# Two attentions with a gate on one core: the projections that come first are reordered and rerouted

## The chip, the cores and the metric

The kernel runs on one core of a Trainium2 chip. Its time is device time in microseconds (us), the median of three executions. Five engines with a queue each work side by side: PE (TensorE, matmuls, which read weights that PEld has loaded), DVE (VectorE), ACT (ScalarE), POOL (GpSimd) and SP (SyncE, here only a queue that issues DMA transfers). ACT and POOL can issue transfers too. An engine takes its instructions in the order in which they are written, and waits at one until its inputs are there.

## The reference

```python
def _A_ref(x, wqkv, wo):          # 32 heads, each with its own keys and values; D = 576, Dh = 18
    qkv = (x @ wqkv).reshape(B, S, 3, H, Dh).transpose(2, 0, 3, 1, 4)
    q, k, v = qkv[0], qkv[1], qkv[2]
    p = softmax(einsum("bhqd,bhkd->bhqk", q, k) * Dh ** -0.5)
    return einsum("bhqk,bhkd->bhqd", p, v).transpose(0, 2, 1, 3).reshape(B, S, D) @ wo

def _B_ref(x, wq, wk, wv, wo):    # 32 query heads share one key and one value
    q = (x @ wq).reshape(B, S, H, Dh).transpose(0, 2, 1, 3)
    k = x @ wk
    v = x @ wv
    p = softmax(einsum("bhqd,bkd->bhqk", q, k) * Dh ** -0.5)
    return einsum("bhqk,bkd->bhqd", p, v).transpose(0, 2, 1, 3).reshape(B, S, H * Dh) @ wo

x = A_x                            # 1 x 2048 x 576, float32
g = sigmoid((x * gate_w).sum(-1, keepdims=True))
return g * _A_ref(x, ...) + (1 - g) * _B_ref(x, ...)
```

## The kernel before

All numbers are float32. Where a matmul needs that accuracy, a matrix is cut into a rounded high part `h` and the rest, the low part `l`, and three products are summed: high by high, high by low, low by high.

**First phase (`project`, L205; the change lies here).** The columns of all query and key weights, of the shared value and of the gate stand side by side in `wall`, cut into 14 tiles (`mt`) of 128 columns. X transposed is 576 by 2048, in four chunks (`c`) of 512 positions, loaded as eight pieces `xs` of 256. A job (`mt`, `c`) is 14 matmuls into one PSUM bank. The contraction over 576 rows has four blocks of 128 and a fifth of 64, which `load5` (L127) loads twice, into both halves of the partitions. ACT rounds weights (`wh`, L133) and X (`xh`, L275); DVE makes the low parts (`wl`, L134; `xl`, L276; and for the fifth block L277, which puts the low part of X into the upper half of `xh`).

The products are kept as float16 pairs, scaled per row by powers of two in `tv`, so that queries and keys are of like size. For that `measure` (L159) takes the largest absolute weight of every column of a tile: a DVE reduction over the row blocks (`wabs`, L162), a PE transpose (L165) and another reduction (L166). `balance` (L168) masks these by what the columns are (`mask`, built in DRAM by small transfers and read back by an element gather), takes the largest of queries and keys and writes `tv` through a dozen small DVE steps and two small PE steps (L176, L183). It is called for the shared-key attention after tiles 0 to 4, and for the other after tiles 5 to 13.

The order: loads of W 0 to 4, then X; five measures; `balance(0, 5)`; then chunk by chunk tiles 0 and 1; then nine measures; `balance(2, 14)`; then tiles 2 to 13, each over its four chunks. A job's bank is evicted right behind its matmuls: ACT writes `ph` (L214) and, for tiles with keys, a copy `pst` (L217); DVE writes `pl` (L220); from tile 0 and the tiles with keys come differences of chunks too (`pd`, `pdh`, `pdl`, L223 to L226). `ph` is stored to DRAM (`qkh`) by ACT's queue, `pl` (`qkl`) by POOL's. `shared_v` (L236) turns the shared value of tile 0 with four PE transposes (L239). At its end the loads of the first keys (`ksb`, `kdb`) and queries (`qs`) wait on POOL.

**Lead and second phase.** The values are projected (`project_v`, L249, matmuls at L252) while the first row maxima are taken; its first matmul follows the last job on PE. Then, for 64 heads, scores, exponentials (ACT, L453), maxima (DVE, L418) and the products with values, in an order written out by hand, and the output product. These parts are the same in both kernels.

Of the kernel before, what the change touches and what calls it, by code (L numbers as in the profile page):

```python
# [49 lines left out]
def gated_mix_kernel(ctx: ExitStack, tc: tile.TileContext, xT, wall, wv, wo, out):  # L50
# [3 lines left out]
    def dma(o, i, eng=None):  # L54
        o, i = (x.bitcast(F32) if x.dtype == F32R else x for x in (o, i))
        return (eng or nc.sync).dma_start(o, i)  # L56
# [52 lines left out]
    def load_k(t, r, eng=None):  # L109
        load_rows(t, r, (0, 1, 0), eng)  # L110
# [13 lines left out]
        if l is not None:  # L124
            eng_l.tensor_tensor(l, src, h.bitcast(F32), op=OP.subtract)

    def load5(t, src):  # L127
        dma(t[:, 0:4, :], src[0:512, :].rearrange("(k p) m -> p k m", p=P))
        dma(t[0:64, 4, :], src[512:576, :])
        dma(t[64:128, 4, :], src[512:576, :])  # L130

    def split_w(st, w, eng_l):
        nc.scalar.activation(w["h"], st, AF.Copy)  # L133
        eng_l.tensor_tensor(w["l"], st, w["h"].bitcast(F32), op=OP.subtract)  # L134

    norm = wpool.tile([P, MT], F32, name="norm", bufs=1)
    tv = wpool.tile([P, MT], F32, name="tv", bufs=1)
    mask = wpool.tile([P, 4, MT], F32, name="mask", bufs=1)
    two = wpool.tile([2, P], F32, name="two", bufs=1)
# [4 lines left out]
    nc.gpsimd.memset(tv, 0.0)  # L144
    mask_d = dram.tile([4, MT * P], F32, name="mask_d")
# [8 lines left out]
    def load_w(mt):  # L154
        st = wpool.tile([P, NKT, P], F32, name="wst", bufs=MT)
        load5(st, wall[mt])
        return st

    def measure(mt, st):  # L159

        a = wpool.tile([P, P], F32, name="wabs")
        nc.vector.tensor_reduce(a, st.rearrange("p k f -> p f k"), axis=AX.X, op=OP.max,  # L162
                                apply_absolute_value=True)
# [4 lines left out]
    def balance(g, n):  # L168

        m = wpool.tile([P, 2, MT], F32, name="bm", bufs=1)  # L170
        for i in range(2):
            nc.vector.tensor_tensor(m[:, i, 0:n], norm[:, 0:n], mask[:, g + i, 0:n], op=OP.mult)
        r = wpool.tile([P, 2], F32, name="br", bufs=1)
        nc.vector.tensor_reduce(r, m[:, :, 0:n], axis=AX.X, op=OP.max)
# [6 lines left out]
        nc.vector.tensor_scalar(dg, ident[0:2, 0:2], x, None, op0=OP.mult)  # L181
        pb = ps_m.tile([P, 512], F32, name="pm")
        nc.tensor.matmul(pb[:, 0:2], two, dg, start=True, stop=True)  # L183
        b = wpool.tile([P, 2], F32, name="bb", bufs=1)
        nc.vector.reciprocal(b[:, 1:2], pb[:, 1:2])
        nc.vector.tensor_tensor(b[:, 0:1], pb[:, 0:1], b[:, 1:2], op=OP.mult)
        e = wpool.tile([P, 2], I32, name="be", bufs=1)
        nc.vector.tensor_single_scalar(e[:, 0:1], b[:, 0:1].bitcast(I32), 24, op=OP.logical_shift_right)
        nc.vector.tensor_scalar(e[:, 1:2], e[:, 0:1], 1.0, 64.0, op0=OP.mult, op1=OP.add)
        nc.vector.tensor_scalar(e[:, 0:1], e[:, 0:1], -1.0, 190.0, op0=OP.mult, op1=OP.add)  # L190
        t = wpool.tile([P, 2], F32, name="bt", bufs=1)
        nc.vector.tensor_single_scalar(t.bitcast(I32), e, 23, op=OP.logical_shift_left)
        nc.vector.tensor_scalar(t, t, LIFT, None, op0=OP.mult)
        for i in range(2):
            nc.vector.scalar_tensor_tensor(tv, mask[:, g + i, :], t[:, i:i + 1], tv, op0=OP.mult, op1=OP.add)

    def prep_w(st):
# [7 lines left out]
    def project(mt, c, w):  # L205

        fp = ps_s.tile([P, 512], F32, name="ps")
        cs = slice(c * 512, (c + 1) * 512)
        for n, (a, b, k, kr) in enumerate(PROJ):
            nc.tensor.matmul(fp, w[a][:kr, k, :], X[b][:kr, k, cs], start=(n == 0), stop=(n == len(PROJ) - 1))  # L210
# [10 lines left out]
        if c == 1 and mt in HAS_K:  # L221
# [2 lines left out]
            dh, dl = (stp.tile([P, 512], F16, name=f"pd{y}", bufs=1) for y in "hl")  # L224
            nc.scalar.activation(dh, d, AF.Copy, scale=t)
            nc.vector.scalar_tensor_tensor(dl, d, t, dh, op0=OP.mult, op1=OP.subtract)  # L226
        dma(qk_d[0][mt * P:(mt + 1) * P, cs], h, nc.scalar)
        dma(qk_d[1][mt * P:(mt + 1) * P, cs], l, nc.gpsimd)
        if c == 1 and mt in HAS_K:
            dma(kd_d[0][mt * P:(mt + 1) * P, :], dh, nc.scalar)  # L230
            dma(kd_d[1][mt * P:(mt + 1) * P, :], dl, nc.gpsimd)
        if mt == 0:
            dma(z_d[cs], st[ROW_G:ROW_G + 1, :], nc.scalar)
            return c, st

    def shared_v(c, st):  # L236
        pv = ps_m.tile([P, 512], F32, name="pm")
        for j in range(4):
            nc.tensor.transpose(pv[:, 18 * j:18 * j + 18],  # L239
# [20 lines left out]
            pass  # L260

    WV = []
    with tc.tile_pool(name="xs", bufs=6, side="right") as xsp:
        W = [load_w(mt) for mt in range(5)]
        XS = []

        def load_x(c):
            XS.append(xsp.tile([P, NKT, 256], F32, name="xs"))
            load5(XS[c], xT[:, 256 * c:256 * c + 256])

        def split_x(c):
            xs = XS[c]
            cs = slice(c * 256, (c + 1) * 256)
            xh = X["h"][:, :, cs]
            nc.scalar.activation(xh, xs, AF.Copy)  # L275
            nc.vector.tensor_tensor(X["l"][:, :, cs], xs[:, 0:4], xh[:, 0:4].bitcast(F32), op=OP.subtract)  # L276
            nc.vector.tensor_tensor(xh[64:128, 4], xs[64:128, 4], xh[64:128, 4].bitcast(F32), op=OP.subtract)  # L277

        for c in range(6):
            load_x(c)  # L280
        WP = [prep_w(W[0])]
        for mt in range(5):
            measure(mt, W[mt])
        balance(0, 5)
        for c in range(2):
            split_x(c)
        WP.append(prep_w(W[1]))
        for c in range(6, 8):
            load_x(c)
        for mt in range(5, MT):  # L290
            W.append(load_w(mt))
        for c in range(4):
            if c < 3:
                split_x(2 * c + 2)
                split_x(2 * c + 3)
            keep = project(0, c, WP[0])
            project(1, c, WP[1])
            shared_v(*keep)
    vwp = ph1.enter_context(tc.tile_pool(name="vwp", bufs=1, side="right"))
    VS = [vwp.tile([P, NKT, 288], F32, name="vwst"), None]  # L300
    load5(VS[0], wv[:, 0:288])

    for b in (SB, MB):
        dma(ksb[b + 54:b + 56, :], ones_r, nc.gpsimd)
    load_k(ksb, ROW_KB, nc.gpsimd)
    load_kd(kdb, ROW_KB, nc.gpsimd)
    load_q(0, nc.gpsimd)

    def project_rest():
        WN = prep_w(W[2])  # L310
        for mt in range(5, MT):
            measure(mt, W[mt])
        balance(2, MT)
        for mt in range(2, MT):
            w = WN
            if mt + 1 < MT:
                WN = prep_w(W[mt + 1])
            for c in range(4):
                project(mt, c, w)
            if mt in (4, 5):  # L320
                load_q(mt - 3, nc.gpsimd)
            if mt in (8, 11):
                hf = (mt - 8) // 3
                WV.append({y: vwp.tile([P, NKT, 288], F32R, name=f"vw{y}{hf}") for y in "hl"})
                split_w(VS[hf], WV[hf], nc.vector)
                if hf == 0:
                    VS[1] = vwp.tile([P, NKT, 288], F32, name="vwst")
                    load5(VS[1], wv[:, 288:576])

    project_rest()  # L330

# [444 lines left out]
```

## Time and profile before

| | us |
|---|---|
| median of three executions | 2733.3 (2733.19 to 2733.45) |
| the profiled execution | 2735.79 |
| its span | 2734.0 |
| PE busy | 2663.3 (97%) |
| DVE busy | 2430.7 (89%) |
| ACT busy | 2384.1 (87%) |
| POOL busy | 231.0 (8%) |
| granted clock of PE, mean | 0.991 |

A busy share is a mean over stages with different limits. The first 240 us, which hold the first phase, have another shape than the rest, and what the change is worth is read there. A row of a timeline gives start, duration, engine, line, instruction, output and input, and in brackets how long the engine stood idle before it and who released it.

### The profile page before, as it was taken

Reading aid. Unit: us, or ns where it says so; the run is one execution under the profiler, and the core shown is the slowest. Engines: PE = TensorE matmul, PEld = TensorE weight load, DVE = VectorE, ACT = ScalarE, POOL = GpSimd, SP = SyncE. Lnnn points to the kernel's source line nnn. Section 1 sums busy time; section 2 is a strip of 40 time slices with the busy share of each in tenths; the row PEclk is TensorE's granted clock in tenths of the full one; section 3 lists DMA queues with packets and bytes.
Section 4 is the critical chain, followed back from the end, with each engine's and each line's share of the span. In section 5 each row is a group of like instructions: output and inputs, shape, how many; then the busy total and the mean of one; then the engine's idle time right before and its main releaser. Section 6 shows DMA issues by size and latency. Waiting matters only on the chain.

```text
span 2734.0 us, 57725 instructions
## 1 busy us (share of the span) xinstructions
PE 2663.3 (97%) x22160; PEld 958.8 (35%) x22160; DVE 2430.7 (89%) x4582; ACT 2384.1 (87%) x4768; POOL 231.0 (8%) x438
## 2 busy tenths in 40 slices
PE   5899999999999999999999999999999999999999
PEld 3688522222222222222222333333333332223444
DVE  5345899999999999999999999999999999998875
ACT  3232499999999999999999999999999999998875
POOL 2221000001000200110110001000100020001000
PEclk9899999999999999999999999999999999999998
DMA  7232100001100100110132112112221122122312
GB/s 197 76 118 90 51 20 20 20 18 53 35 17 23 54 27 20 45 43 20 30 66 85 40 51 84 54 40 57 72 66 47 44 61 64 39 64 88 89 36 94
DMA packets 135321, 151.49 MB, mean 55 GB/s; under 512 B 55709, under 2 KB 104765, under 8 KB 133846
## 3 DMA queue, kind: packets, MB, share of 16 engines
q1 hardware_dynamic: 116156, 123.59, 16.2%
q10 hardware_dynamic: 14120, 13.65, 1.5%
q0 software_dynamic: 4768, 10.56, 1.2%
q8 instruction: 174, 2.85, 0.5%
q14 instruction: 103, 0.84, 0.1%
HBM read 92.02 MB, written 46.45 MB: 51 GB/s over the span
## 4 chain that ended last, share of the span: by engine, by line
ACT 54%; PE 37%; DVE 6%; DMA 2%; SPq 1%; issue 1%; DVEq 0%; ACTq 0%
ACT pt L453 48%; PE acc L459 12%; PE ps L446 11%; ACT xb L412 6%; PE ps L210 6%; PE pm L575 4%; DVE mx L418 3%; PE ps L252 2%; PE pm L409 2%; SPq L56 1%; DVE oe L469 1%; DVE junk L415 1%; DMA xs<-xT 0%; DVE oacc L629 0%; DVE oacc L583 0%
## 5 line engine op out<-in xcount | busy, mean ns | idle before, releaser
L453 ACT ACTIVATE pt<-ps 128x512 f32<-128x512 f32 x4052 | 2093.1, 637 | 68.4 <-PE pm L409 60.2
L418 DVE TENSOR_REDUCE mx<-pm 128x1 f32<-128x512 f32 x3096 | 1940.2, 682 | 89.5 <-PE pm L409 74.6
L446 PE MATMUL ps<-qs,ksb 56*128 56x512 f16 x2688 | 818.4, 380 | 10.8
L409 PE MATMUL pm<-ksb,qs 54*128 54x512 f16 x2364 | 738.5, 383 | 2.6 <-DVE mx L418 1.6
L459 PE MATMUL acc<-pt,vb 128*19 128x512 f32 (+1 forms) x6136 | 592.3, 458 | 1.9
L459 PE MATMUL acc<-pt,vg 128*19 128x256 f32 (+1 forms) x5664 | 579.5, 481 | 2.3 <-DVE oe L469 0.5
L409 PEld LDWEIGHTS <-qs 54*128 54x128 f16 x4096 | 330.0, 93 | 248.1 <-issue 195.2
L446 PE MATMUL ps<-qs,ksa 56*128 56x512 f16 x1364 | 404.4, 379 | 4.8 <-ACT pt L453 1.3
L446 PEld LDWEIGHTS <-ksb 56*128 56x128 f16 x2688 | 175.0, 94 | 622.5 <-issue 573.9
L409 PE MATMUL pm<-ksa,qs 54*128 54x512 f16 x1232 | 384.8, 382 | 0.6 <-ACT xb L412 0.4
L415 DVE CUSTOM_DVE_ANT_0 junk<-pm,xb 128x512 bf16<-128x512 f32 x500 | 339.9, 680 | 0.0
L412 ACT ACTIVATE xb<-pm 128x512 f32<-128x512 f32 x500 | 316.5, 633 | 0.0
L446 PEld LDWEIGHTS <-ksa 56*128 56x128 f16 x1408 | 89.3, 94 | 328.9 <-issue 299.0
L459 PEld LDWEIGHTS acc<-pt,vb 128*19 128x19 f32 x6136 | 104.1, 96 | 223.7 <-issue 206.6
L459 PEld LDWEIGHTS acc<-pt,vg 128*19 128x19 f32 x5664 | 96.0, 97 | 222.9 <-issue 204.9
L428 POOL TENSOR_SCALAR mt<-mt 128x32 f32<-128x32 f32 x64 | 18.6, 290 | 1616.4 <-DVE mt L426 1616.4
L214 ACT ACTIVATE ph<-ps,tv 128x512 f16<-128x512 f32 x56 | 38.5, 687 | 122.0 <-PE ps L210 114.5
L409 PE MATMUL pm<-kdb,qs 54*128 54x512 f16 x372 | 141.5, 380 | 0.0
L220 DVE SCALAR_TENSOR_TENSOR pl<-ps,tv,ph 128x512 f16<-128x512 f32 x56 | 42.0, 751 | 93.8 <-ACT ph L214 75.4
L210 PE MATMUL ps<-xh,wh 128*128 128x512 f32 x280 | 76.4, 403 | 3.3 <-DVE xh L277 2.6
L210 PE MATMUL ps<-xh,wl 128*128 128x512 f32 x280 | 75.1, 399 | 0.0
L469 DVE COPY oe<-acc 128x512 f32<-128x512 f32 x63 | 43.6, 692 | 30.0 <-PE acc L459 29.4
(123 smaller groups left out, 1253.8 us busy)
## 6 DMA issues: line engine op xcount, KB each, us to landing
qs<-qkh SPq DMA_DIRECT2D x244, 72.0 KB
qs<-qkl SPq DMA_DIRECT2D x122, 72.0 KB
onh<-oh SPq DMA_DIRECT2D x32, 256.0 KB
onl<-ol SPq DMA_DIRECT2D x32, 256.0 KB
oih<-onh SPq DMA_DIRECT2D x16, 512.0 KB
oil<-onl SPq DMA_DIRECT2D x16, 512.0 KB
ot<-oe SPq DMA_DIRECT2D x220, 36.0 KB
R<-r_d SPq DMA_DIRECT2D x55, 144.0 KB
```

The lines of the kernel that those rows point to most:

```text
L210: nc.tensor.matmul(fp, w[a][:kr, k, :], X[b][:kr, k, cs], start=(n == 0), stop=(n == len(PROJ) - 1))
L220: nc.vector.scalar_tensor_tensor(l, fp, t, h, op0=OP.mult, op1=OP.subtract)
L252: nc.tensor.matmul(fp[:, 0:288], X[b][:kr, k, st_ * P:(st_ + 1) * P], w[a][:kr, k, :], start=(n == 0), stop=(n == len(PROJ) - 1))
L409: nc.tensor.matmul(pm, qs[u % 3][b:b + 54, i * P:(i + 1) * P], k, start=True, stop=True)
L412: nc.scalar.activation(MX["x", u, i], pm, AF.Relu)
L415: nc.vector.tensor_tensor_reduce(junk, pm, MX.pop(("x", u, i)), 1.0, -3e38, op0=OP.add, op1=OP.max, accum_out=MX[u][:, i, c:c + 1])
L418: nc.vector.tensor_reduce(MX[u][:, i, c:c + 1], pm, axis=AX.X, op=OP.max)
L446: nc.tensor.matmul(ps, kst(u)[b:b + 56, i * P:(i + 1) * P], qs[u % 3][b:b + 56, c * 512:(c + 1) * 512], start=True, stop=True)
L453: nc.scalar.activation(pt, ps, AF.Exp, scale=SCALE / LIFT ** 2)
L459: nc.tensor.matmul(acc[32 * j:32 * j + 19, a:b], v_of(u, i), PT[u, i, j][:, a:b], start=(i == 0 and a == 0), stop=(i == 15), skip_group_ch ...
L469: nc.vector.tensor_copy(oe, acc)
L575: nc.tensor.matmul(fp[:, 0:288], o[b][:r, t, s2 * P:(s2 + 1) * P], w[a][:r, t, 288 * hf:288 * hf + 288], start=(n == 0), stop=(n == 3 * nt ...
```

## The change

- Three tiles go through X chunk by chunk instead of two (`JOBS`). W 0, X 0, W 1, X 1, W 2 are loaded in this order, X 0 by ACT's queue. For the first chunk the three tiles are multiplied a 256-column half at a time. 18 matmuls on zeros run ahead of them, and a small ACT instruction ahead of the first weights.
- `measure` falls into `measure_b` (tiles 0 to 4: one largest value a partition for the queries and one for the shared keys) and `measure_a` (tiles 4 to 13: a value a column and partition, kept), both without PE. `balance` does the rest over partitions at once, in three parts between which jobs 4 and 5 (or 14 and 15) stand. The first two chunks' six banks (three `ps`, three `pm`) are held until the first balance has ended.
- From then on the eviction of a job is written behind the matmuls of the next (`late`, `flush`); banks alternate by threes between the two pools. The measures of tiles 4 to 13 stand between the evictions of jobs 7 to 13.
- The 64-row block is loaded once; ACT writes its rounded weights to both halves.
- The mask is loaded by rows and turned by four PE transposes.
- `ph`, `pdh` and the gate's row are stored by POOL, as `pl` is; from tile 3 on, POOL makes the low weights.
- The loads of the first keys and queries stand between jobs of tiles 4 to 7.

The number of jobs (56) and of matmuls in one (14) is as before.

```diff
-PROJ = [("h", "h", k, 128) for k in range(NKT)] + [("h", "l", k, 128) for k in range(NKT - 1)] + \
-       [("l", "h", k, 128) for k in range(NKT)]
+PROJ = [("h", "h", k, 128) for k in range(NKT - 1)] + [("l", "h", k, 128) for k in range(NKT - 1)] + \
+       [("h", "l", k, 128) for k in range(NKT - 1)] + [("h", "h", NKT - 1, 128), ("l", "h", NKT - 1, 64)]
...
-    def load5(t, src):
-        dma(t[:, 0:4, :], src[0:512, :].rearrange("(k p) m -> p k m", p=P))
-        dma(t[0:64, 4, :], src[512:576, :])
-        dma(t[64:128, 4, :], src[512:576, :])
+    def load5(t, src, eng=None):
+        dma(t[:, 0:4, :], src[0:512, :].rearrange("(k p) m -> p k m", p=P), eng)
+        dma(t[0:64, 4, :], src[512:576, :], eng)
...
-        nc.scalar.activation(w["h"], st, AF.Copy)
-        eng_l.tensor_tensor(w["l"], st, w["h"].bitcast(F32), op=OP.subtract)
+        nc.scalar.activation(w["h"][:, 0:4], st[:, 0:4], AF.Copy)
+        for b in (0, 64):
+            nc.scalar.activation(w["h"][b:b + 64, 4], st[0:64, 4], AF.Copy)
+        eng_l.tensor_tensor(w["l"][:, 0:4], st[:, 0:4], w["h"][:, 0:4].bitcast(F32), op=OP.subtract)
+        eng_l.tensor_tensor(w["l"][0:64, 4], st[0:64, 4], w["h"][0:64, 4].bitcast(F32), op=OP.subtract)
...
-    dma(mask, mask_d.rearrange("g (m p) -> p g m", p=P), nc.gpsimd)
+    dma(mask_r, mask_d.rearrange("g (m p) -> m g p", p=P), nc.gpsimd)
+
+    def turn_mask():
+        pt = ps_m.tile([P, 512], F32, name="pm")
+        for g in range(4):
+            nc.tensor.transpose(pt[:, MT * g:MT * g + MT], mask_r[:, g, :], ident[0:MT, 0:MT])
+        nc.vector.tensor_copy(mask, pt[:, 0:4 * MT].rearrange("p (g m) -> p g m", m=MT))
...
-    def measure(mt, st):
-        a = wpool.tile([P, P], F32, name="wabs")
-        nc.vector.tensor_reduce(a, st.rearrange("p k f -> p f k"), axis=AX.X, op=OP.max,
+    def size(n, st):
+        for k0, k1, p in ((0, 4, P), (4, 5, 64)):
+            nc.vector.tensor_reduce(n[0:p, k0 // 4:k0 // 4 + 1], st[0:p, k0:k1], axis=AX.XY, op=OP.max,
+                                    apply_absolute_value=True)
+    def measure_b(mt, st):
+        if mt == 0:
+            size(norm_b[:, 0, 0:2], st[:, :, ROW_KB:ROW_KB + DH])
+        f0, f1 = max(ROW_Q - P * mt, 0), min(ROW_Q + DH * H - P * mt, P)
+        size(norm_b[:, 1, 2 * mt:2 * mt + 2], st[:, :, f0:f1])
+    def measure_a(mt, st):
+        o = norm_a[:, P * (mt - 4):P * (mt - 3)]
+        nc.vector.tensor_reduce(o, st[:, 0:4].rearrange("p k f -> p f k"), axis=AX.X, op=OP.max,
                                 apply_absolute_value=True)
-        pt = ps_m.tile([P, 512], F32, name="pm")
-        nc.tensor.transpose(pt[:, 0:P], a, ident)
-        nc.vector.tensor_reduce(norm[:, mt:mt + 1], pt[:, 0:P], axis=AX.X, op=OP.max)
+        a = wpool.tile([64, P], F32, name="wabs", bufs=1)
+        nc.vector.tensor_reduce(a, st[0:64, 4:5].rearrange("p k f -> p f k"), axis=AX.X, op=OP.max,
+                                apply_absolute_value=True)
+        nc.vector.tensor_tensor(o[0:64], o[0:64], a, op=OP.max)
...
-        w = {y: wpool.tile([P, NKT, P], F32R, name=f"w{y}") for y in "hl"}
-        split_w(st, w, nc.vector)
+        w = {y: wpool.tile([P, NKT, P], F32R, name=f"w{y}", bufs=4) for y in "hl"}
+        split_w(st, w, eng or nc.gpsimd)
...
-        dma(qk_d[0][mt * P:(mt + 1) * P, cs], h, nc.scalar)
+        dma(qk_d[0][mt * P:(mt + 1) * P, cs], h, nc.gpsimd)
         dma(qk_d[1][mt * P:(mt + 1) * P, cs], l, nc.gpsimd)
...
+    def project(n, hold=False):
+        mt, c = JOBS[n]
+        fp = bank(n // 3 % 2)
+        products(fp, WP[mt], 512 * c, 0, 512)
+        if not hold:
+            flush()
+        late.append(lambda: evict(mt, c, fp))
+        if mt == 0:
+            late.append(lambda: late.append(lambda: shared_v(c)))
...
+        FP = [bank() for mt in range(3)]
+        for i in range(2):
+            for mt in range(3):
+                products(FP[mt], WP[mt], 0, 256 * i, 256 * i + 256)
+        for mt in range(3):
+            measure_b(mt, W[mt])
+        for c in (2, 3):
             split_x(c)
+        turn_mask()
...
+        for mt in (3, 4):
+            measure_b(mt, W[mt])
+        project(3, hold=True)
+        bal = balance(0)
+        for n in (4, 5):
+            next(bal)
+            project(n, hold=True)
+        run(bal)
+        for mt in range(3):
+            evict(mt, 0, FP[mt])
+            if mt == 0:
+                for c in (4, 5):
+                    split_x(c)
+        flush()
+        WP.append(prep_w(W[3]))
+        shared_v(0)
+        for n in range(6, 12):
+            if n == 8:
+                for c in (6, 7):
+                    split_x(c)
+            project(n)
+            for mt in range(*AT.get(n, (0, 0))):
+                measure_a(mt, W[mt])
```

What the change moves, in the order of the instructions, at three places.

PE, the start of the first phase. Before: five transposes of measures (L165), the balance (L176, L183), then tiles 0 and 1 on chunk 0.

```order
L165 MATMUL pm<-ident,wabs 128x128 x5
L176 MATMUL pm<-ident,br 2x128
L183 MATMUL pm<-bd,two 128x2
L210 MATMUL ps<-xh,wh 128x512 x5
L210 MATMUL ps<-xl,wh 128x512 x4
L210 MATMUL ps<-xh,wl 128x512 x5
```

Now, from the end of job 4 on: a step of the balance (L205), job 5 (L240, banks `pm`), the other step (L213), the shared value's transposes (L276) and job 6.

```order
L240 MATMUL pm<-xh,wh 128x512
L240 MATMUL pm<-xh,wl 128x512
L205 MATMUL pm<-ident,br 2x128
L240 MATMUL pm<-xh,wh 128x512 x4
L240 MATMUL pm<-xh,wl 128x512 x4
L240 MATMUL pm<-xl,wh 128x512 x4
L240 MATMUL pm<-xh,wh 128x512
L240 MATMUL pm<-xh,wl 128x512
L213 MATMUL pm<-bd,two 128x2
L276 MATMUL pm<-ident,pst 128x18 x4
L240 MATMUL ps<-xh,wh 128x512 x4
```

The products no longer stand behind the balance; the first eviction does.

DVE, around the measures of the later tiles. Before: behind the last eviction of tiles 0 and 1 (L220), the low weights of tile 2, and nine pairs of a measure and its second reduction.

```order
L220 SCALAR_TENSOR_TENSOR pl<-ps,tv,ph 128x512 x2
L242 COPY vb<-pm 128x4x18
L134 TENSOR_TENSOR wl<-wst,wh 128x640
L162 TENSOR_REDUCE wabs<-wst 128x128
L166 TENSOR_REDUCE norm<-pm 128x1
L162 TENSOR_REDUCE wabs<-wst 128x128
L166 TENSOR_REDUCE norm<-pm 128x1
```

Now, from the eviction of job 6 (L254) on: the measures of tiles 4 and 5 (L186 to L191), then the last two pieces of X (L333, L334), then job 7 and the next measure.

```order
L254 SCALAR_TENSOR_TENSOR pl<-ps,tv,ph 128x512
L186 TENSOR_REDUCE norm_a<-wst 128x128
L189 TENSOR_REDUCE wabs<-wst 64x128
L191 TENSOR_TENSOR norm_a<-norm_a,wabs 64x128
L186 TENSOR_REDUCE norm_a<-wst 128x128
L189 TENSOR_REDUCE wabs<-wst 64x128
L191 TENSOR_TENSOR norm_a<-norm_a,wabs 64x128
L333 TENSOR_TENSOR xl<-xs,xh 128x4x256
L334 TENSOR_TENSOR xh<-xs,xh 64x256
L333 TENSOR_TENSOR xl<-xs,xh 128x4x256
L334 TENSOR_TENSOR xh<-xs,xh 64x256
```

The measures moved in between the evictions, two of them ahead of the last pieces of X.

POOL, around the loads of the third head's queries (`qs_94`). Before: the low stores (`qkl`, and `kdl` for a difference) and the loads.

```order
L56 DMA qkl<-pl 128x512 x2
L56 DMA kdl<-pdl 128x512
L56 DMA qkl<-pl 128x512 x2
L56 DMA qs_94<-qkh 18x2048 x2
L56 DMA qs_94<-qkl 18x2048
```

Now: both stores of each job, and the low weights of the next tile (L136, L137) between them.

```order
L56 DMA kdh<-pdh 128x512
L56 DMA kdl<-pdl 128x512
L56 DMA qkh<-ph 128x512
L56 DMA qkl<-pl 128x512
L136 TENSOR_TENSOR wl<-wst,wh 128x512
L137 TENSOR_TENSOR wl<-wst,wh 64x128
L56 DMA qkh<-ph 128x512
L56 DMA qkl<-pl 128x512
L56 DMA qs_94<-qkh 18x2048 x2
L56 DMA qs_94<-qkl 18x2048
```

POOL's queue now holds all stores of a job and half of the weight split.

More of the change, by code (lines that the diff above doesn't have):

```diff
@@ L304, in gated_mix_kernel @@
         dma(ksb[b + 54:b + 56, :], ones_r, nc.gpsimd)
-    load_k(ksb, ROW_KB, nc.gpsimd)
-    load_kd(kdb, ROW_KB, nc.gpsimd)
-    load_q(0, nc.gpsimd)
     def project_rest():
[L310 to L328, printed above, removed]
+        bal = None
@@ new lines, in project_rest @@
+        for n in range(12, len(JOBS)):
+            mt, c = JOBS[n]
+            if c == 0 and mt + 1 < MT:
+                WP.append(prep_w(W[mt + 1]))
+            project(n)
+            for m in range(*AT.get(n, (0, 0))):
+                measure_a(m, W[m])
+            if n == 13:
+                bal = balance(2)
+            if n in (13, 14):
+                next(bal)
+            if n == 15:
+                run(bal)
+            if c == 0:
+                if mt == 4:
+                    load_k(ksb, ROW_KB, nc.gpsimd)
+                    load_kd(kdb, ROW_KB, nc.gpsimd)
+                if mt == 5:
+                    load_q(0, nc.gpsimd)
+                if mt in (6, 7):
+                    load_q(mt - 5, nc.gpsimd)
+                if mt in (7, 10):
+                    hf = (mt - 7) // 3
+                    VS[hf] = vwp.tile([P, NKT, 288], F32, name="vwst")
+                    load5(VS[hf], wv[:, 288 * hf:288 * hf + 288])
+                if mt in (9, 12):
+                    hf = (mt - 9) // 3
+                    WV.append({y: vwp.tile([P, NKT, 288], F32R, name=f"vw{y}{hf}") for y in "hl"})
+                    split_w(VS[hf], WV[hf], nc.vector)
@@ L330, in gated_mix_kernel @@
+        for f in list(late):
+            f()
     project_rest()
```

108 lines of the change are left out of this document (66 added, 42 removed).

## The prediction

> A difference of 0.2% (5.5 us of 2733) is about what a measurement of this kernel can tell from no change.
>
> **What bounds the kernel now.** I read the page's slices first, then the busy time by stretch, then the chain of waits of the first 320 us. The slices show where TensorE is not full:
>
> ```profile
> PE   5899999999999999999999999999999999999999
> DVE  5345899999999999999999999999999999998875
> ACT  3232499999999999999999999999999999998875
> ```
>
> Each digit is a slice of 68 us. Only PE's first three are below 9; from the fifth on ACT and DVE are full, and that part is not edited. The stretches (busy us of PE, PEld, DVE, ACT, POOL; granted clock; DMA share; GB/s):
>
> ```profile
> 0.00:23.80 23.80, 3.27 (x8) 1.49 (x8) 10.35 (x24) 4.58 (x5) 7.37 (x19) 1.00 0.77 164
> 23.80:238.50 214.70, 192.82 (x812) 154.45 (x813) 98.59 (x149) 70.67 (x99) 49.81 (x94) 0.94 0.39 123
> 60.00:62.00 2.00, 0.00 (x0) 0.00 (x0) 1.36 (x2) 1.23 (x2) 1.97 (x4) 0.61 0.95 244
> ```
>
> The projections end at 238.5, DVE and ACT below half busy, Pool a quarter. In the chain (start, us, what) PE's stretches and what separates them:
>
> ```profile
> 22.95 5.08 DMA xs<-xT
> 28.52 7.91 PE ps L210 x24
> 57.50 4.07 DMA wst<-wall
> 61.59 5.93 DMA vwst<-wv
> 67.56 1.23 DVE wabs L162
> 82.02 156.70 PE ps L210 x672
> 238.72 3.73 PE ps L252 x28
> ```
>
> The last 48 of the 56 products are back to back: 672 matmuls in 156.70 us. PE waits in two places: until 23.8 for weights, X and the first balance, and from 57.7 to 82 for nine measures and the second balance. The timeline shows both, and the clock:
>
> ```profile
> 6.57 1.28 ACT L133 ACT_TABLE_LOAD   x1 [6.57 <-DMA wst<-wall]
> 23.83 2.07 PE L210 MATMUL ps<-xh,wh 128*128 128x512 f32 x4 [0.66 <-ACT xh L275]
> 57.24 0.42 PE L239 MATMUL pm<-ident,pst 18*128 18x18 f32 x4
> 81.44 0.58 PE L183 MATMUL pm<-bd,two 2*128 2x2 f32 x2 [0.80 <-DVE bd L181]
> 81.95 2.50 PE L210 MATMUL ps<-xh,wh 128*128 128x512 f32 x5
> 82.06 0.17 DVE L185 RECIPROCAL bb<-pm 128x1 f32<-128x1 f32 x1 [0.67 <-PE pm L183]
> 83.42 0.50 DVE L195 SCALAR_TENSOR_TENSOR tv<-mask,bt,tv 128x14 f32<-128x14 f32 x2
> 87.94 1.32 PE L210 MATMUL ps<-xh,wh 128*128 128x512 f32 x5
> ```
>
> The job at 81.95 takes 6.0 us to 87.94, at half clock. Taking its excess out, a warm job of 14 matmuls costs (156.70 - 2.8)/48 = 3.2 us, so a cold start costs 2.8. All 56 need 179 us; the rest of 238.7 is what the change can reach, some 59 us.
>
> **The change part by part.** Durations of one instruction, from the groups kept apart by shape (busy total, mean ns):
>
> ```profile
> L162 DVE TENSOR_REDUCE wabs<-wst 128x128 f32<-128x640 f32 x14 | 17.1, 1223 | 0.0
> L134 DVE TENSOR_TENSOR wl<-wst,wh 128x640 fp32r<-128x640 f32 x14 | 11.5, 824 | 10.8 <-ACT wh L133 10.7
> L276 DVE TENSOR_TENSOR xl<-xs,xh 128x1024 fp32r<-128x1024 f32 x8 | 9.8, 1224 | 1.9 <-ACT xh L275 1.7
> L277 DVE TENSOR_TENSOR xh<-xs,xh 64x256 fp32r<-64x256 f32 x8 | 3.4, 422 | 0.2
> L220 DVE SCALAR_TENSOR_TENSOR pl<-ps,tv,ph 128x512 f16<-128x512 f32 x56 | 42.0, 751 | 93.8 <-ACT ph L214 75.4 <-ACT pst L217 18.4
> L226 DVE SCALAR_TENSOR_TENSOR pdl<-pd,tv,pdh 128x512 f16<-128x512 f32 x10 | 7.5, 752 | 7.9 <-ACT pdh L225 7.9
> L214 ACT ACTIVATE ph<-ps,tv 128x512 f16<-128x512 f32 x56 | 38.5, 687 | 122.0 <-PE ps L210 114.5 <-DMA wst<-wall 5.1 <-PE pm L239 2.1
> L217 ACT ACTIVATE pst<-ps 128x512 f32<-128x512 f32 x13 | 7.7, 590 | 0.0
> L133 ACT ACTIVATE wh<-wst 128x640 fp32r<-128x640 f32 x14 | 10.2, 734 | 4.2 <-ACT ph L214 3.2 <-DMA wst<-wall 0.9
> L275 ACT ACTIVATE xh<-xs 128x1280 fp32r<-128x1280 f32 x8 | 10.0, 1269 | 14.8 <-DMA xs<-xT 13.9 <-ACT ph L214 1.0
> L56 POOL DMA_DIRECT2D qkl<-pl x56 | 30.5, 545 | 161.0 <-DVE pl L220 150.8 <-DVE vb L242 5.7 <-DVE pdl L226 4.1
> L125 POOL TENSOR_TENSOR ol<-ot,oh 128x512 fp32r<-128x512 f32 x32 | 40.9, 1277 | 5.3 <-DMA onl<-ol 3.8
> L239 PE MATMUL pm<-ident,pst 18*128 18x18 f32 x16 | 1.7, 215 | 0.0
> ```
>
> Front. The table load moves ahead of the weights. They land at 6.6, their split (0.73, in three pieces 1.1) ends at 7.7 and X's first piece (1.27) at 9.0, so the first product starts at 9.0 instead of 23.8. X now shares this time with the weights; 384 columns of 576 floats, 0.9 MB, must have come:
>
> ```profile
> 4.00:6.00 2.00, 0.00 (x0) 0.00 (x0) 0.00 (x0) 0.00 (x0) 1.63 (x4) 1.00 0.69 183
> 22.00:24.00 2.00, 0.72 (x3) 0.67 (x4) 1.01 (x7) 1.49 (x2) 0.00 (x0) 1.00 1.11 294
> ```
>
> At 294 GB/s from 4 us on this costs nothing; at 183 the later steps slip by 1 to 4 us (two pieces and three weights, 896 columns, 2.06 MB, at 15.3 instead of 11). I take the fast one, since the row at 4 has weights alone, at the pace at which SP issued them.
>
> Chunk 0 is done in six half groups of 14 matmuls on 256 columns. Half a job is 1.6 us; the L252 row gives 1.87 for 14 on 288 columns (3.73 for 28). I take 1.75: to 19.5, with the mask's turn 20.0. DVE keeps ahead: three weight splits of 0.82 and two X pieces of 1.22 + 0.42 from 7.4 on end at 13.2, before the second half's 14.3. Then come five tiles' measures without a transpose (three of them first: 1480 elements at no more than L162's 1.9 ns, 2.8 us, and four 64-row ones of some 0.25) and two X pieces, at 20.3; job 3 needs them at 21.8. The 18 empty products before 9.0 only set the clock. Jobs 3 to 5: 9.6, and 0.4 for a transpose: 30.0.
>
> The stall that stays. Nothing can be evicted before the balance, whose last part follows job 5. Its PE part (0.58) and DVE tail (82.06 to 83.92: 1.9) end at 32.5. Then ACT does 0.69 + 0.59 for the first bank and the two X pieces of chunk 2 (1.27 each, now in two instructions: 2.6) before job 6 can start: 36.4. PE stands 5.8 us. In the stretch 60:62 the mean clock is 0.61, so it fell to half near 60.4, 2.8 us after the last matmul (57.24 + 0.42); so here too it falls, and job 6 starts cold: 2.8, or 2.4 as in the 24 matmuls of 7.91 (5.5 warm). I take 2.6; without the fall it is 0. The Trainium skill ("TensorE: Matmul & The Clock Gate", Part 1) has the gate close after an idle window of about 3.4 us that runs free of the kernel, which would close it here as well, and a window at half clock costs half of it, an estimate of 1.7 us, by which the sum were 0.9 lower; the trace's 2.4 to 2.8 decides.
>
> Jobs 6 to 55: 50 x 3.2 = 160.3 (3.206 before rounding). What lies beside them: ACT 0.69 a job, now one job late and with no job waiting for it, since a bank returns after six. In the way: three times four turns of V (0.4 each), 1.2; the second balance's two small PE steps, 1.0; and DVE. From 32.5 it owes, until job 9 needs chunk 3 at 50.8, seven low parts (5.3), the difference and its low part (1.5), four X pieces (6.6), two measures (0.98 for 512 of L162's 640 elements and two small steps of some 0.25: 1.45 each) and copies (0.4), 16.7 us in 18.3 with hand-overs from ACT: wait 0 to 3, I take 1. Then six low parts (4.5), eight measures (11.6) and two reductions with a copy (1.7) until the second balance's transpose after job 14, at 69.6; from 51.8 on they end at 69.6 too: wait 0 to 2, I take 0.5. Together 3.7. So the nine measures' 14 us of waiting, the loads ahead of them and the second cold start go.
>
> Pool. It takes over the high stores and the weights' low parts. A tile has ten issues (5.45), 1.28 for the low part and 0.25 to 1.3 for its 64 rows: 7.0 to 8.0 of 12.8 us. Its last store frees the bank's copy three jobs later:
>
> ```profile
> qkl<-pl POOLq DMA_DIRECT2D x56, 128.0 KB, 2.1
> ```
>
> At 2.1 us to land there are 6 us of slack; a tile's low part is needed four jobs after it is made. Cost: nothing, while Pool needs less than 3.2 us a job. The 64-row loads drop a third of the issues of SP.
>
> Sum: 36.4 + 2.6 + 160.3 + 3.7 = 203.0 instead of 238.7: 35.7 us less. The rest follows with the same instructions. The profiled execution took 2735.79 (its span 2734.0), 2.5 above the median of 2733.3; from the median: 2697.6, say 2698.
>
> **The rivals.** *DVE's debt.* If ACT's hand-overs or the measures are longer, X's last pieces come late, job 9 waits and the clock falls again. Price: 5 us of wait, 2.8 cold, 2 more at the second balance, 10 us: 2708. For it: 16.7 of 18.3 us; against: later there is slack.
>
> *Pool locked out by DVE.* If Pool's issue must wait for the DVE instruction that runs, a store takes up to 0.545 + 1.22. Two stores (3.5) and a quarter of a low part (0.4) make 3.9 us a job, 0.7 over PE's, for the dozen jobs in which DVE is full: 8.8 us, 2707. The row that bears on it:
>
> ```profile
> 61.38 1.22 DVE L162 TENSOR_REDUCE wabs<-wst 128x128 f32<-128x640 f32 x1
> 61.59 0.52 POOL L56 DMA_DIRECT2D ksb<-qkh  x1
> ```
>
> This issue lies wholly inside a DVE reduction and takes no longer than others, so I give it little. The Trainium skill ("SBUF — State Buffer", "SBUF: two separate sides") warns of such a lock, in which DMAs issued from GpSimd wait while VectorE runs a two-port instruction; by that rule the stores were better left on ACT's queue, and no row here shows it.
>
> *The front fed late.* With all loads at 183 GB/s and latencies on top, chunks 0 and 1 end 10 us later, with two cold starts between: 15.6, 2713.
>
> *Pool the bound (slower).* All stores now stand in one queue. If a high store there costs not 0.545 but what the mask's gather cost Pool,
>
> ```profile
> L56 POOL DMA_DIRECT2D mask<-mask_d x1 | 2.6, 2555 | 2.6 <-DMA mask_d<-zo 2.6
> ```
>
> a tile with five of them needs 12.8, 2.7 for the others and 1.6 for the low part, 17.1 us, 4.3 a job: 50 jobs take 54 us more, 2752. It decides from 0.71 us a job above 3.2, where the gain is gone (35.7/50). Against it: that gather had 4-byte pieces, and the same store of the low part takes 0.545.
>
> **How the numbers follow.** Forecast 0.66, alone 2693 (no fall of the clock, no wait of DVE, half groups at 1.6) to 2707 (slow loads 4, waits at their upper ends 3.5, 2 for hand-overs between engines). DVE's debt 0.13, Pool locked 0.07, front late 0.06; the change without effect, since something else starts the next stage at 238.7, 0.02; Pool the bound 0.06. The range 2688 to 2713 adds below one cold start (2.8) that a shift in time may spare the second stage, and leaves out the last two and some of the tails. Faster 0.92, same 0.02, slower 0.06.
>
> **What would show it.** Right: first product near 9, one hole of 5 to 6 us near 31 with half clock behind it, the first product of V (now L289) near 203, Pool's stores at 0.55. Wrong: holes between jobs 16 and 55, Pool above 3 us a job, or the second phase longer than 2495 us.

## The result, and the profile after

The changed kernel takes 2725.8 us (median of 9 runs, 2725.0 to 2726.2) against 2733.3 (9 runs of the kernel before on the same chip): a ratio of 0.9972, 95% interval 0.9962 to 0.9982. That is 7.5 us less, where 35 were forecast (2698, range 2688 to 2713). The profiled execution took 2726.2, its span 2724.3.

The slices of the page, PE, DVE and ACT. PE's first slice has an 8 for a 5, the second a 9 for an 8:

```profile
PE   8999999999999999999999999999999999999999
DVE  6335899999999999999999999999999999998865
ACT  4332599999999999999999999999999999998875
```

So TensorE is busy nearly everywhere, and the time is still only 7.5 us shorter. The chain of waits of the first 330 us (start, us, what) shows what it is busy with:

```profile
10.22 11.20 PE ps L240 x76
...
38.46 6.22 PE ps L240 x14
...
52.67 10.94 PE pm L240 x42
...
97.12 10.94 PE pm L240 x42
...
206.52 10.94 PE pm L240 x42
217.46 7.29 PE ps L240 x28
224.75 4.49 PE ps L289 x28
```

Three jobs (42 products) take 10.94 us, one 3.647, and from job 16 on nothing stands between them. The kernel before took 3.208 for the same 14 products (from 87.94 to 238.72 in the rows of the prediction, 47 jobs). V's first product starts at 224.7, not at 203: 14 us of the 35.7 are left. Two groups of V take 4.49 instead of 3.73 as well, so that the rest, from V's first product to the end of the span, grew from 2495.3 to 2499.6 us.

Where a job loses time is seen in the timeline of PE and of its weight loads (PEld), one job of the kernel after:

```profile
99.02 1.10 PE L240 MATMUL pm<-xl,wh 128*128 128x512 f32 x4
99.95 0.39 PE L240 MATMUL pm<-xh,wh 128*128 128x512 f32 x1
100.27 0.49 PE L240 MATMUL pm<-xh,wl 64*128 64x512 f32 x1
100.69 1.20 PE L240 MATMUL pm<-xh,wh 128*128 128x512 f32 x4
101.73 1.10 PE L240 MATMUL pm<-xh,wl 128*128 128x512 f32 x4
```

```profile
99.72 0.19 PEld L240 LDWEIGHTS pm<-xh,wh 128*128 128x128 f32 x1
100.27 0.18 PEld L240 LDWEIGHTS pm<-xh,wl 64*128 64x128 f32 x1 [0.36 <-issue]
100.69 0.76 PEld L240 LDWEIGHTS pm<-xh,wh 128*128 128x128 f32 x4 [0.24 <-issue]
```

Read the two together. The weights of the 128-row product at 99.95 are loaded from 99.72 on, while the products before it run. Those of the 64-row product are loaded only at 100.27, together with their product, after an idle time of the loader of 0.36; and the next 128-row weights wait again, 0.24. From one start to the next it is 0.32 us into the 64 rows and 0.42 out of them, where neighbours of 128 rows have 0.23, and the four products behind take 1.04 (100.69 to 101.73) instead of 0.93: some 0.4 us more in all. These 64-row products are the change's: its last entry of PROJ has 64 rows, the kernel before had 128 in all 14.

### The profile page after: what moved, and what is told of

It is laid out like the page before. It is cut to its first block, busy times and chain, and to the rows that moved or that the text cites. A ratio compares the mean times of both kernels' runs of the same rounds, so it can differ in the third digit from the quotient of the medians.

```text
span 2724.3 us, 57935 instructions
## 1 busy us (share of the span) xinstructions
PE 2689.0 (99%) x22210; PEld 957.2 (35%) x22210; DVE 2421.9 (89%) x4589; ACT 2389.5 (88%) x4809; POOL 285.7 (10%) x531
## 4 chain that ended last, share of the span: by engine, by line
ACT 50%; PE 40%; DVE 6%; DMA 2%; issue 1%; SPq 1%; POOL 0%; DVEq 0%; ACTq 0%; POOLq 0%
ACT pt L555 45%; PE acc L561 13%; PE ps L548 11%; ACT xb L514 6%; PE pm L677 4%; PE ps L240 4%; PE pm L240 4%; DVE mx L520 3%; PE ps L289 3%; PE pm L511 1%; SPq L56 1%; DMA R<-r_d 1%; DVE oe L571 1%; DVE junk L517 1%; DVE oacc L731 0%
## 5 line engine op out<-in xcount | busy, mean ns | idle before, releaser
L248 ACT ACTIVATE ph<-ps,tv 128x512 f16<-128x512 f32 x29 | 19.8, 686 | 67.3 <-PE ps L240 43.2
L292 ACT ACTIVATE vst<-ps 128x288 f32<-128x288 f32 x32 | 13.2, 412 | 67.4 <-PE ps L289 67.4
L248 ACT ACTIVATE ph<-pm,tv 128x512 f16<-128x512 f32 x27 | 18.4, 686 | 54.5 <-PE pm L240 40.6
L254 DVE SCALAR_TENSOR_TENSOR pl<-pm,tv,ph 128x512 f16<-128x512 f32 x27 | 20.1, 749 | 48.8 <-ACT ph L248 38.7
```

The lines of the kernel that those rows point to most:

```text
L248: nc.scalar.activation(h, fp, AF.Copy, scale=t)
```

## The experiments

Theory T: a change between 128 and 64 rows keeps the next weights from being loaded beside the running product. Rival M: the 64-row product is slow by itself. Rival O: the jobs are slow from another part of the change (Pool's stores, evictions a bank late, DVE's work). Each ratio is to the kernel before, in the same runs on the same chip.

**The last product on 128 rows.** The low part of W's fifth block is then written in both halves.

```diff
-       ... ("h", "h", NKT - 1, 128), ("l", "h", NKT - 1, 64)]
+       ... ("h", "h", NKT - 1, 128), ("l", "h", NKT - 1, 128)]
...
-    eng_l.tensor_tensor(w["l"][0:64, 4], st[0:64, 4], ...)
+    for b, n in ((0, 64), (64, 64)):
+        eng_l.tensor_tensor(w["l"][b:b + n, 4], st[0:n, 4], ...)
```

> The changed kernel with its last product of a group on 128 rows, as the kernel before had it: the low part of W's fifth block is written in both halves (one more 64x128 subtraction per tile of W). Everything else of the change stays. Theory T (each change between 128 and 64 rows empties TensorE's pipeline, 0.44 us for the two changes of a job): a job of 3.2 us instead of 3.647, 53 x 0.44 = 23 less there, some 1.5 in the half groups, 4 to 5 in V's products: 2693 to 2699 us. Theory M (the 64-row product is slow by itself, whatever stands beside it): the same 2693 to 2699. Theory O (the jobs are slow from something else of the change: stores on Pool, evictions a bank late, DVE's work): a job stays at 3.6 and the time at 2726.

2702.0 us, ratio 0.9875 (0.9860 to 0.9889). Its chain:

```profile
36.31 6.23 PE ps L241 x14
...
189.07 9.80 PE pm L241 x42
198.88 6.53 PE ps L241 x28
205.41 3.70 PE ps L290 x28
```

A job takes 3.267, V's first product starts at 205.4, and what follows it takes 2494.1 (2499.6 before this edit). O falls. It comes out 3 us above the range that was expected, and 3.267 is not 3.208: 0.06 us a job are still missing.

**Every second job in reversed order**, so that two 64-row products of neighbouring jobs stand side by side.

```diff
-        for n, (a, b, k, kr) in enumerate(PROJ):
+        for n, (a, b, k, kr) in enumerate(PROJ[::-1] if back else PROJ):
...
-        products(fp, WP[mt], 512 * c, 0, 512)
+        products(fp, WP[mt], 512 * c, 0, 512, back=n > 5 and n % 2 == 1)
```

> The changed kernel with the products of every second job from job 7 on in reversed order, so that two 64-row products of neighbouring jobs stand side by side: the same instructions, half the changes of row count in jobs 6 to 55. Theory T: 50 x 0.22 = 11 us less, 2715, two jobs in some 6.85 us. Theory M: no change, 2726, two jobs in 7.29. Theory O: 2726.

2720.5 us, ratio 0.9943 (0.9928 to 0.9957). Three jobs take 10.36, one 3.453, half way between 3.647 and 3.267: as many 64-row products, half the changes, half the loss. M falls here, and with the next two runs. The time is still 5 us above the 2715 of theory T: a change cost 0.19 us instead of 0.22, and the reversed job 9 needs the low part of X's fifth block earlier, waits 1.5 us for it and runs at half clock behind the wait.

**Two 64-row products in a group**, the second being the high part of the fifth block by the high part of W; side by side, and then apart. Both leave out the low part of X's fifth block.

```diff
-       ... ("h", "h", NKT - 1, 128), ("l", "h", NKT - 1, 64)]
+       ... ("h", "h", NKT - 1, 64), ("l", "h", NKT - 1, 64)]
```

> The changed kernel with both products of the fifth block on 64 rows, side by side (this leaves out of the result the low part of X's fifth block): twice the 64-row products, the same number of changes of row count. Theory T: a job as in the changed kernel, 3.65, time 2726. Theory M: 0.44 us more a job, 4.09, and 5 more in V's products: 2754. Theory O: 2726.

2725.1 us, ratio 0.9961 (0.9947 to 0.9975), a job of 3.64.

```diff
 PROJ = [("h", "h", k, 128) for k in range(NKT - 1)] + \
+       [("h", "h", NKT - 1, 64)] + \
...
-       ... ("h", "h", NKT - 1, 64), ("l", "h", NKT - 1, 64)]
+       ... ("l", "h", NKT - 1, 64)]
```

> The same two 64-row products as in the run before this one (the low part of X's fifth block is left out again), but not side by side: one after the first four products, one at the end of the group, so four changes of row count a job instead of two. Theory T: 0.44 us more a job than with the two side by side, 4.09, and 4 to 5 more in V's products: 2754. Theory M: the same as with the two side by side. Theory O: 2726.

2760.2 us, ratio 1.0088 (1.0073 to 1.0103). Row of its chain: 42 products in 12.08, a job 4.03.

```profile
226.38 12.08 PE pm L241 x42
```

The same two products cost 0.39 us a job more as soon as 128-row products stand between them. The changes cost, not the products. The forecast of 2754 was 6 us low, since V's groups lost more than the 4 to 5 us assumed: what follows V's first product took 2512.0 instead of 2499.5, 0.39 for each of 32 groups.

**One part of the change alone in the kernel before**: its last product on 64 rows.

```diff
-       [("l", "h", k, 128) for k in range(NKT)]
+       [("l", "h", k, 128) for k in range(NKT - 1)] + [("l", "h", NKT - 1, 64)]
```

> One part of the change alone in the kernel before: the last product of a group on 64 rows instead of 128, everything else as before. Theory T (each pair of changes of row count costs 0.38 us a job, the difference between the changed kernel's job and that of the run with 128 rows): 56 x 0.38 = 21 us more in the projections, 5 more in V's products: 2735 + 27 = 2762, a job of 3.6. Theory O (the jobs of the changed kernel are slow because of other parts of it): the time of before, 2735.

2760.3 us, ratio 1.0096 (1.0081 to 1.0111): 26 us more, from this one number. A job takes 3.63 (from 89.68, the second, to V's first product at 260.12: 47 jobs in 170.4), 0.42 more than the 3.208 without this edit.

**96 rows.** As the first run, with 32 rows fewer in the last product.

```diff
-       ... ("l", "h", NKT - 1, 128)]
+       ... ("l", "h", NKT - 1, 96)]
...
-    for b, n in ((0, 64), (64, 64)):
+    for b, n in ((0, 64), (64, 32)):
```

> The changed kernel with its last product on 96 rows (the low part of W's fifth block is written in a further 32 rows). If any change of row count empties the pipeline, 2726 and a job of 3.65 as in the changed kernel. If only 64 rows or fewer against more count as a change, 2702 and a job of 3.27 as in the run with 128 rows.

2701.6 us, ratio 0.9880 (0.9866 to 0.9895). Start to start stays near 0.23 us on both sides (timeline of PE):

```profile
123.16 0.39 PE L241 MATMUL ps<-xh,wh 128*128 128x512 f32 x1
123.39 0.40 PE L241 MATMUL ps<-xh,wl 96*128 96x512 f32 x1
123.63 1.10 PE L241 MATMUL ps<-xh,wh 128*128 128x512 f32 x4
```

So it isn't any change in the count: 96 beside 128 is free, 64 beside 128 is not. The Trainium skill ("TensorEngine Tiling (Array Packing)", section "Tiling Modes") says that a change of the array's tiling mode, not of the tile alone, drains TensorE, and lists 64 rows as a mode of its own and none with 96. The traces fit this, and price a pair of changes at 0.38 us, which the page doesn't. No row names the mode, but in the program as built the products of 64 and 54 rows have a tile of 64 rows, and those of 96 and 128 rows one of 128. The Trainium skill also says ("TensorE: Matmul & The Clock Gate", Part 3) that weight loads overlap running products only where their row groups differ, though the same part has them pulled ahead into a background weight buffer as well. Here 128-row loads (0.19 us) lie beside 128-row products in every job, and it is the change that ends the overlap.

**The first balance a job earlier**, on top of the run with 128 rows, to test the account of the stall near 33 us.

```diff
-        project(3, hold=True)
         bal = balance(0)
-        for n in (4, 5):
-            next(bal)
-            project(n, hold=True)
+        next(bal)
+        project(3, hold=True)
+        next(bal)
+        for c in (4, 5):
+            split_x(c)
+        project(4, hold=True)
         run(bal)
+        project(5, hold=True)
...
-            if mt == 0:
-                for c in (4, 5):
-                    split_x(c)
```

> The run with 128 rows, and the first balance a job earlier: its reduction ahead of job 3, its transpose behind job 3, its end behind job 4, with X's fifth and sixth piece split on ACT and DVE while job 4 runs; job 5 then covers the tail. If the prediction's account of the stall is right (5.4 us in which PE stands, and 2.6 of half clock behind it, nothing else late): job 6 follows job 5 without a gap, 8 us less than with 128 rows alone, 2694. If the stall only moves (chunk 2 or DVE's debt is late next): 2697 to 2702.

2697.6 us, ratio 0.9867 (0.9852 to 0.9882): 4 of the 8 us (V's first product at 201.2 instead of 205.4). The timeline of PE shows the stall gone from job 6 (0.37 left) and half of it back a job later; DVE's row names the releaser, a store (the wait in brackets):

```profile
31.17 1.20 PE L241 MATMUL ps<-xh,wh 128*128 128x512 f32 x4 [0.37 <-DVE pl L255]
...
37.09 0.43 PE L277 MATMUL pm<-ident,pst 18*128 18x18 f32 x4 [2.39 <-DVE pd L258]
37.45 2.08 PE L241 MATMUL ps<-xh,wh 128*128 128x512 f32 x4
```

```profile
35.59 0.75 DVE L255 SCALAR_TENSOR_TENSOR pl<-pm,tv,ph 128x512 f16<-128x512 f32 x1 [3.16 <-DMA qkl<-pl]
```

Six banks are evicted at once into three buffers; the fourth waits for the first stores to land, and V's next turn on PE behind it.

**The old order of the products** on top of that, to look for the 0.06 us a job.

```diff
-PROJ = [("h", "h", k, 128) for k in range(NKT - 1)] + [("l", "h", k, 128) for k in range(NKT - 1)] + \
-       [("h", "l", k, 128) for k in range(NKT - 1)] + [("h", "h", NKT - 1, 128), ("l", "h", NKT - 1, 128)]
+PROJ = [("h", "h", k, 128) for k in range(NKT)] + [("h", "l", k, 128) for k in range(NKT - 1)] + \
+       [("l", "h", k, 128) for k in range(NKT)]
```

> The run before this one with the products in the order of the kernel before (high by high five times, high W by low X four times, low W by high X five times). A job of the run with 128 rows takes 3.266, one of the kernel before 3.208. If the order makes these 0.058 us: a job of 3.21 and 50 x 0.058 = 2.9 us less than the run before this one, 2691. If not: 3.266, 2694, or up to 1 us more, since X's low part is needed earlier in the front.

2699.8 us, ratio 0.9876 (0.9860 to 0.9893): a job still takes 3.267, and V's first product is 2 us later, since PE waits 2.2 for X's low parts, which this order needs sooner. The order isn't it.

**Four store buffers instead of three** (the run with the early balance, products in the new order).

```diff
-        h = stp.tile([P, 512], F16, name="ph")
-        l = stp.tile([P, 512], F16, name="pl")
+        h = stp.tile([P, 512], F16, name="ph", bufs=4)
+        l = stp.tile([P, 512], F16, name="pl", bufs=4)
```

> The run with the first balance a job earlier, with four buffers for each of the two parts of an evicted bank instead of three. There six banks were evicted at once into three buffers, the fourth waited for a store to land (DVE 3.2 us), the second turn of V behind it, and PE stood from 34.5 to 37.1 and ran at half clock behind it, 4.1 us in all. With a fourth buffer: 4.1 us less, 2693.5, jobs 7 to 11 without a hole over 0.5 us. If the fifth and sixth bank then hold up job 9 or 10 in the same way: 2696 to 2698.

2696.1 us, ratio 0.9859 (0.9844 to 0.9873). The hole at 34.5 is gone (V's turn at 35.02 waits for nothing), but with the jobs earlier, X's last pieces are now late. This row is the second third of job 9:

```profile
46.22 1.20 PE L241 MATMUL pm<-xl,wh 128*128 128x512 f32 x4 [1.65 <-DVE xl L334]
```

This is the wait that the prediction priced as DVE's debt. It is 0.2 us while the stall ahead of it stands (the run with 128 rows, the last run below), grows once the stall is gone, and takes back 1.65 of the 4.1.

**W's tiles 128 bytes lower.** One scratch tile is 128 bytes longer, so that W's split tiles, and all that lies below them, move by 128 bytes in each partition: they start 160 bytes past a multiple of 512, as in the kernel before, and not 288, as in the changed one. X stays in place, and the instructions are the same.

```diff
-        a = wpool.tile([64, P], F32, name="wabs", bufs=1)
+        a = wpool.tile([64, P + 32], F32, name="wabs", bufs=1)[:, 0:P]
```

> The run with four buffers, with one scratch tile 128 bytes longer, so that W's split tiles start at 160 bytes past a multiple of 512 in each partition, as in the kernel before, instead of 288. The same instructions. In the kernel before a product starts every 0.2286 us, in the run with 128 rows every 0.2333, in either order of the products. If the place of the weights makes it: 0.229 and 50 x 0.06 = 3 us less than with four buffers. If not: the same time to 0.5 us, and the cause of the 0.06 us a job stays open.

2694.8 us (2693.1 to 2695.8, the run before it 2695.9 to 2696.5), ratio 0.9853 (0.9838 to 0.9868), the best of all. Its chain, beside the same place of the run with four buffers:

```profile
181.22 9.61 PE pm L241 x42
190.83 6.42 PE ps L241 x28
197.25 3.69 PE ps L290 x28
```

```profile
183.24 9.80 PE pm L241 x42
193.04 6.53 PE ps L241 x28
199.57 3.69 PE ps L290 x28
```

42 products in 9.61, a product every 0.2288 us instead of 0.2333. The place of the tiles makes the 0.06 us a job. V's groups (3.69) don't feel it. V's first product comes 2.3 us earlier and the median is 1.4 lower, where 3 were forecast: up to the second balance (job 14 at 65.3 against 65.1) nothing is gained, since PE waits for DVE there.

**The high stores back on ACT's queue**, on top of the run with four buffers.

```diff
-        dma(qk_d[0][mt * P:(mt + 1) * P, cs], h, nc.gpsimd)
+        dma(qk_d[0][mt * P:(mt + 1) * P, cs], h, nc.scalar)
```

(and so for the key differences and the gate's rows.)

> The run with four buffers, with the stores of the high parts back on ACT's queue, as in the kernel before (56 of them, the key differences and the gate's rows too). If Pool's queue or a lock between DVE and Pool costs anything: up to 8 us less than with four buffers. If not: the same time to 1 us; ACT then issues 56 stores more.

2700.2 us, ratio 0.9874 (0.9858 to 0.9891): 4 us slower than on Pool. A steady job is the same 3.267; V's first product is 3 us later, from the stretch after the balance, where ACT evicts six banks: each issue adds 0.35 us to ACT's queue there, and PE waits for it (PE's waits; behind the first of them job 9 runs at half clock):

```profile
PE pm L241 <- ACT xh L332: 1.7, 1, 1.7
PE pm L277 <- DVE pd L258: 1.2, 1, 1.2
```

So Pool's stores are a gain, and no lock shows.

**The two causes out of the changed kernel, and nothing else**: 128 rows and the longer scratch tile.

> The changed kernel with only the two causes found taken out: the last product on 128 rows, and the scratch tile 128 bytes longer, so that W's split tiles lie 160 bytes past a multiple of 512. The first balance and the store buffers are as in the changed kernel. If these two are all that the prediction missed: a job of 3.20, the first product of V at 205.4 - 2.9 = 202.5 (the prediction said 203), and 2699 against 2733.3 for the kernel before, or 36 us below whatever that kernel takes in the same runs. If something else is missing, the first product of V stays at 204 or later.

2698.8 us (2698.3 to 2699.3), ratio 0.9867 (0.9851 to 0.9883). Its chain:

```profile
186.36 9.61 PE pm L241 x42
195.97 6.41 PE ps L241 x28
202.39 3.69 PE ps L290 x28
```

V's first product starts at 202.4 (forecast 203), and the rest takes 2494.8 (2495.3 in the kernel before). That is 35.5 us less than the kernel before took in the same runs (2734.3), where the prediction had 35.7.

## Why the prediction was wrong, step by step

**What failed: "Jobs 6 to 55: 50 x 3.2 = 160.3".** The step counted 14 products as before and took the job's price over unchanged. The last one had gone from 128 rows to 64, and W's tiles had moved. A job was 3.647: 0.380 from the change of rows (3.647 - 3.267), 0.063 from the place of the tiles (9.80 against 9.61 for three). The split holds for this order of taking them out; in the kernel before, the rows alone cost 0.42. Over 50 jobs the two are 19.0 and 3.2 us, 22.2 together. The half groups and jobs 3 to 5 have 64-row products too: job 6 started at 38.46 instead of 36.4, 2.1 late (36.31 with 128 rows). What lies beside the jobs took 1.5 instead of 3.7. So V's first product missed 203 by 21.7. The 64-row products in V cost 5.5 more behind it (2499.6 against 2494.1).

The warning was in the trace of before, which has products of 54 rows among V's groups. There too the loader stands, 0.16 going in and 0.42 coming out (timeline of PEld, kernel before):

```profile
241.49 0.72 PEld L252 LDWEIGHTS ps<-vwl,xh 128*128 128x128 f32 x5
242.38 0.11 PEld L409 LDWEIGHTS <-qs 54*128 54x128 f16 x4 [0.16 <-issue]
242.91 0.70 PEld L252 LDWEIGHTS ps<-vwh,xh 128*128 128x128 f32 x5 [0.42 <-issue]
```

**"The rest follows with the same instructions"** failed for the same reason: V's groups read the same PROJ, so the lead isn't the same in both kernels, as the description of the kernel before has it. The prediction itself named a second phase over 2495 us as a sign of an error; it was 2499.6.

**Front: right.** The first product starts at 8.96 (9.0 forecast), nothing is fed late (284 GB/s from 10 to 20 us), and DVE keeps ahead but for 0.2 us at 10.2. A half group took 2.0 instead of 1.75, the rows again: 1.59 with 128 rows (16.11 to 17.70 in that run). The rival of a slow front falls.

**The stall: right, in place and size.** PE stood from 33.0 to 38.5, 5.4 us (5.8 forecast), broken by one turn of V; job 6 then ran cold, 6.2 us, some 2.5 over a warm job (2.6 forecast). With the two causes out it lies from 30.5 to 35.9 (30.6 to 36.4 forecast). Removing it in the run with the early balance gave its price back in part, the rest having moved to the next wait.

**What lies beside the jobs: right, a little high.** No wait at job 9 in the changed kernel, where the longer jobs give DVE time; 0.2 and 0.3 at job 9 and at the second balance with the two causes out, where I had 1 and 0.5, and 3.4 in all (3.7 forecast).

**Pool: right.** A row of the changed kernel's groups:

```profile
L56 POOL DMA_DIRECT2D qkh<-ph x56 | 30.8, 549 | 65.7 <-ACT ph L248 65.4 <-issue 0.3
```

0.549 us a store (0.55 forecast), and Pool waits for ACT ahead of them, 65 us in all; of PE's queues the weight loader waits for Pool once, 0.4 us. Neither the slower rival (2752) nor the lock (2707) shows; the run with ACT's stores says that the old queue would have been the dearer one.

So the account of what the change removes was sound, as the last run shows at 2698.8 and term by term; the job's price was not.

## What to carry to other kernels

An instruction count prices nothing while the shapes differ: before a job's time is carried over, look in the trace for a product of that row count next to one of another, and read start to start, with the weight loads beside it. Among products of 128 rows, one that could do with 64 was better run on 128 here (2702.0 against 2725.8 us), or at least kept next to another of 64. And once a stall is removed, expect the wait behind it (buffers of stores, then late pieces of X) to take back a part.

## What the runs showed of the hardware

- A pair of changes between 128 and 64 rows costs 0.38 us with 512 columns (0.42 in the kernel before), and 0.39 with the 288 columns of V, where the first group, from 224.68 to 226.92, takes 2.24 for 14 products of 0.1325. In the changed kernel V loses only 5.5 us in 32 groups: behind two groups in three stand 54-row products, which are a change of rows in either kernel, and the loader waits 0.16 us for them behind 128 rows and not at all behind 64. 96 rows beside 128 cost nothing.
- Moving the weight tiles by 128 bytes in their partitions (from 288 to 160 past a multiple of 512) changed the pitch of 512-column products from 0.2333 to 0.2288 us, in both runs that did it. It split all kernels so: 0.229 in the four at 160 (the kernel before, the same with 64 rows, and these two), 0.233 in the ten at 288. Half jobs of 256 columns took 0.114 or 0.1175 a product in either place, and V's groups of 288 the same in both. Which of the moved tiles does it, and by what, stays open, and no third place was tried.
- The clock fell behind holes of only 2.4, 1.7 and 1.5 us. The first is in the run with the early balance (PE's busy time first, then PEld, DVE, ACT, POOL, and the granted clock after them):

```profile
35.00:36.00 1.00, 0.00 (x0) 0.00 (x0) 0.41 (x1) 0.00 (x0) 0.13 (x1) 1.00 1.11 372
36.00:37.00 1.00, 0.00 (x0) 0.00 (x0) 0.94 (x2) 0.03 (x1) 0.36 (x1) 1.00 1.01 386
37.00:38.00 1.00, 0.91 (x5) 0.85 (x6) 0.27 (x1) 1.00 (x2) 0.19 (x2) 0.65 0.55 203
...
39.00:40.00 1.00, 1.00 (x4) 0.81 (x3) 1.00 (x4) 0.95 (x4) 1.00 (x3) 0.50 0.54 188
40.00:41.00 1.00, 1.00 (x4) 0.76 (x4) 0.08 (x1) 1.00 (x3) 1.00 (x3) 0.65 0.33 109
```

It was at half from some 37.3 to 40.7. The others, with PE's row that ends the hole and the stretch behind it, are in the run with ACT's stores and in the one with reversed jobs:

```profile
45.28 1.49 PE L241 MATMUL pm<-xh,wh 128*128 128x512 f32 x4 [1.71 <-ACT xh L332]
47.00:48.00 1.00, 1.00 (x4) 0.66 (x2) 0.94 (x3) 0.27 (x1) 0.00 (x0) 0.50 0.39 124
```

```profile
54.15 0.75 PE L240 MATMUL pm<-xh,wh 128*128 128x512 f32 x1 [1.54 <-DVE xh L334]
55.00:56.00 1.00, 1.00 (x4) 0.71 (x4) 1.00 (x3) 0.00 (x0) 0.54 (x1) 0.50 0.58 66
```

The hole of 1.65 us in the run with four buffers left no cold job behind it: the 34 products from 46.22 on took 8.20 us, 0.241 each. So the length of the hole alone doesn't decide, and what else does isn't shown. All three spells at half clock lasted some 3.4 us, and the one behind the long stall of the changed kernel 6.8 (37.2 to 44.0). The Trainium skill ("TensorE: Matmul & The Clock Gate", Part 1) has the gate close after an idle window of about 3.4 us; here holes of 1.5 to 2.4 us were enough, if not each of them.
